# Attention backward on one core: first loads split over two queues, the second head's projections moved forward, dwq and dx tiles reordered

## The chip, the cores and the metric

The kernel runs on one NeuronCore of a Trainium2 chip. A core has a matrix engine (TensorE, PE in the profile, with its weight loads as PEld), a vector engine (VectorE, DVE), an activation engine (ScalarE, ACT), GpSimd (POOL), and SyncE (SP), which here only issues DMAs. Each engine runs its own instructions in the order in which the program puts them and waits on semaphores for the others. Sixteen DMA engines move data between HBM and the on-chip memory; DMAs are issued from the queue of an engine. TensorE writes to PSUM, which here is a pool of eight banks; VectorE or ScalarE evict the banks.

The metric is the device time of one execution in microseconds (us), the median of several runs. Lower is better.

## The reference

Two independent attention layers A and B, each with x (8 batches x 96 tokens x 640), a key and a value cache (8 x 32 heads x 512 x 128), and weights wq (640 x 4096) and wo (4096 x 640). All tensors are bfloat16. What is computed is the output and the gradient of all ten inputs:

```python
q = (x @ wq).reshape(B, Sq, H, Dh).transpose(0, 2, 1, 3)
scores = jnp.einsum("bhqd,bhkd->bhqk", q, k_cache) * (Dh ** -0.5)
p = softmax(scores, axis=-1)
o = jnp.einsum("bhqk,bhkd->bhqd", p, v_cache)
y = o.transpose(0, 2, 1, 3).reshape(B, Sq, H * Dh) @ wo
# out = concat([y_A, y_B], axis=-1); vjp of out with grad_out gives dx, dk, dv, dwq, dwo of A and of B
```

## The kernel before, in words

**Blocks, heads, batches.** Layer A is block 0, layer B is block 1. In a block the kernel goes through 32 heads, in a head through 8 batches; a pair of head and batch is one step of the inner pipeline. All work is put into an emitter with a tick and a slot, sorted by both, and only then issued. Head `h` of a block starts at tick `c0t = tick0 + 8*h` (tick0 is 13 for A and 269 for B); the text calls `c0t + k` the tick at offset k of that head. A framework adds the semaphores and may move an instruction a little within what the data allow; SyncE's DMAs and GpSimd's work are pinned to the program's order, except the very first loads.

**The inner pipeline (one step per tick).** `c_ld` loads K and V of two batches; `c_xt` transposes them by DMA, or, for the first heads, `c_s1` transposes K on TensorE. `c_s2a`: scores `S_ps` on TensorE, their negated row maximum `negm` on VectorE. `c_s2b`: exponential `E_sb` on ScalarE with the row sums. `c_s3a`, `c_s3b`: reciprocal `rinv` on VectorE, `P_sb` on GpSimd. A tick later P is transposed (`x_ps<-ident,P_sb`), evicted by ScalarE (`PT_sb`), and `dV_ps` is made; then the head's output (`x_ps<-PT_sb,V_sb`), `dP_ps` and `dl_ps`, from which VectorE makes `dS_sb`; then the transposes of dS (`dst_ps`), evicted by VectorE (`dST_sb`), `dK_ps`, and `x_ps<-dST_sb,K_sb` for dQ. ScalarE evicts `dK_sb`, `dV_sb`, `PT_sb` and the head's O and dQ (`OD`). In the profile the start of `S_ps` marks a tick: there are 512 of them.

**Work by head, laid between the batches.** `pA`, `pA2` load wq (two heads at once) and wo. `pB` transposes wo and wq of the head on TensorE (`woT_ps`, `wqT_ps`; woT is evicted by ScalarE, wqT by VectorE). `pC(h, 0, si)` is the projection Q and `pC(h, 1, si)` the projection of the gradient (`dOT_h`), each in a piece of 512 and one of 256 tokens, five matmuls a piece (`q_ps`). `pD` transposes them by batch (`n_ps`, to `dOnat_h` and `Qnat_h`). `qA` transposes O and dQ back (`nat_ps`, to `Onat` on ScalarE, 768 columns, and `dQnat` on VectorE). `qB` makes dwo from Onat, in two pieces of six matmuls, one evicted by ScalarE, one by VectorE. `qD` makes dwq of a pair of heads: five units of 6 matmuls of 256 columns (`dwq_ps`), each evicted by VectorE into `dwq_sb`, which has one buffer, and stored by `qD_st` one tick after the last unit. `gU` adds up the output (`which` 0) and dx (`which` 1) over groups of five heads, in six token tiles t of a 512- and a 128-column piece; in B the last group has two heads, and its dx tiles are written to `gT` and stored one by one (tiles 0 and 2 go by ScalarE and GpSimd, the rest by VectorE).

**Where the five dwq units go** is planned: every piece of work by head adds its TensorE time, less 0.8 of its ScalarE time, to its tick's planned load, and a pair `h` (odd) puts each unit at the least loaded offset of 18 to 29 from its head, at most two in one (lines 639 to 649). The last pair of a block has fixed offsets.

**The start** (block A, head 0). SyncE's queue issues x tiles 0 to 3 as one DMA, wo of head 0, wq of heads 0 and 1, K, x tiles 4 and 5, g in two DMAs, then V and K. TensorE runs 32 warm-up matmuls, transposes x tiles 0 to 3, wo and wq, projects Q, and so on; g's six transposes come after the first S.

Of the kernel before, what the change touches and what calls it, by code (L numbers as in the profile page):

```python
# [11 lines left out]
BF16 = mybir.dt.bfloat16  # L12
# [30 lines left out]
SL_HEAD = 90  # L43
# [3 lines left out]
OFF = dict(ldk=-5, ldv=-4, kt=-3, vt=0, s2=3, s3=3, s4=4, s5=5, s6=6, s7=7, s8=8)  # L47
HK = dict(pA=-10, pA2=-9, pB=-3, pC0=[-2, 0], pC1=[-1, 0], pD1=1, pD0=2, qA0=18, qA1=17, qA1e=21, qDw=(18, 29), qB=[19, 20], qD=[(18, 0, 2), (19, 2, 4), (21, 4, 5)])
# [8 lines left out]
def build_block(tc, em, tick0, blk, x, kc, vc, wq, wo, g_all, out_all, dx, dk, dv, dwq, dwo, ident, ones, pools, HG=6, first=True, groups=None):  # L57
    nc = tc.nc
    B, Sq, D = x.shape
    _, H, Sk, Dh = kc.shape  # L60
    assert Dh == 128 and Sk % 128 == 0 and D % 128 == 0
    T = B * Sq
    assert T % 128 == 0
    TT = T // 128
# [10 lines left out]
    NG = len(groups)  # L75
    GH0 = [sum(groups[:i]) for i in range(NG)]
    tsplits = []
    t0 = 0
# [17 lines left out]
    wq_v = wq.rearrange("(c p) n -> p c n", p=128)  # L96
    dwq_v = dwq.rearrange("(c p) n -> p c n", p=128)

    const, ps, kvp, wk, hd, hst, grp = (pools[k] for k in ("const", "ps", "kvp", "wk", "hd", "hst", "grp"))

    def bank(shape, dt, name):
        return ps.tile(shape, dt, name=name, tag="bank")

    S = {}
# [9 lines left out]
    def pinned(ins):  # L114
        return tc.keep_in_program_order(ins)
# [25 lines left out]
    def setup_nat(which_, t0, t1):  # L141
        def f():
            key = "x_nat" if which_ == 0 else "g_nat"
            src_flat = x_flat if which_ == 0 else g_flat
            if t0 == 0:
                S[key] = const.tile([128, TT, D], BF16, name=key, bufs=1)
            nc.sync.dma_start(S[key][:, t0:t1], src_flat.rearrange("(t p) d -> p t d", p=128)[:, t0:t1])
            if first and which_ == 0 and t0 == 0:
                pA2(0)()
                pA(0)()  # L150
        return f
# [6 lines left out]
    def evac(eng, dst, src, sc=None):  # L158
        if eng == "act":
            nc.scalar.activation(dst, src, ACT.Identity, scale=(1.0 if sc is None else sc))  # L160
        else:
            if sc is None:
                nc.vector.tensor_copy(dst, src)  # L163
            else:
                nc.vector.tensor_scalar(dst, src, float(sc), None, op0=ALU.mult)
# [21 lines left out]
    def pA(h):  # L187
        def f():
            start = first and h == 0
            if h % 2 == 0:  # L190
                wq_p = hd.tile([128, DC, 256], BF16, name="wq_p", bufs=2)
                with nc.allow_non_contiguous_dma(reason="wq slice of two heads"):
                    if start:
                        nc.sync.dma_start(wq_p[:], wq_v[:, :, h * 128:(h + 2) * 128])
                    else:
                        pinned(nc.sync.dma_start(wq_p[:], wq_v[:, :, h * 128:(h + 2) * 128]))
            else:
                wq_p = HS[(blk, h - 1)]["wq_p"]
            HS.setdefault((blk, h), {}).update(wq_p=wq_p, wq_h=wq_p[:, :, (h % 2) * 128:(h % 2 + 1) * 128])
        return f  # L200

    def pA2(h):
        def f():
            wo_h = hst.tile([128, D], BF16, name="wo_h", bufs=HG + 3)
            ld = nc.sync.dma_start(wo_h[:], wo[h * 128:(h + 1) * 128, :])
            if not (first and h == 0):
                pinned(ld)
            HS.setdefault((blk, h), {})["wo_h"] = wo_h
        return f

    def pB(h):
        def f():
            st = HS[(blk, h)]
            woT_ps = bank([128, DC * 128], BF16, "woT_ps")
            for c in range(DC):
                nc.tensor.transpose(woT_ps[:, c * 128:(c + 1) * 128], st["wo_h"][:, c * 128:(c + 1) * 128], ident[:])  # L216
            woT_h = hd.tile([128, DC * 128], BF16, name="woT_h", bufs=1)
            evac(EV["pB0"], woT_h[:], woT_ps[:])
            st["woT_h"] = woT_h
            wqT_ps = bank([128, DC * 128], BF16, "wqT_ps")  # L220
            for c in range(DC):
                nc.tensor.transpose(wqT_ps[:, c * 128:(c + 1) * 128], st["wq_h"][:, c, :], ident[:])  # L222
            wqT_h = hst.tile([128, D], BF16, name="wqT_h")
            evac(EV["pB1"], wqT_h[:], wqT_ps[:])
            st["wqT_h"] = wqT_h
            st["slot"] = (blk * H + h) % OD.shape[2]
            st["OT_h"] = OD[:, 0, st["slot"]]
            st["dQT_h"] = OD[:, 1, st["slot"]]
            st["QT_h"] = hd.tile([128, T], BF16, name="QT_h")
            st["dOT_h"] = hd.tile([128, T], BF16, name="dOT_h")  # L230
        return f

    def pC(h, which, si):
        def f():
            st = HS[(blk, h)]
            (t0, w) = tsplits[si]
            if which == 0:
                dst = st["QT_h"]
                lhs = lambda c: st["wq_h"][:, c, :]
                rhsT = S["xT"]  # L240
                sc = scale
            else:
                dst = st["dOT_h"]
                lhs = lambda c: st["woT_h"][:, c * 128:(c + 1) * 128]
                rhsT = S["gT"]
                sc = None
            q_ps = bank([128, w], F32, "q_ps")
            for c in range(DC):
                nc.tensor.matmul(q_ps[:], lhs(c), rhsT[:, c, t0:t0 + w], start=(c == 0), stop=(c == DC - 1))  # L249
            evac(EV["pC%d%d" % (which, si)], dst[:, t0:t0 + w], q_ps[:], sc)  # L250
        return f
# [249 lines left out]
    def qD_st(h):  # L501
        def f():
            with nc.allow_non_contiguous_dma(reason="dwq slice of two heads"):
                pinned(nc.sync.dma_start(dwq_v[:, :, (h - 1) * 128:(h + 1) * 128], HS[(blk, h)]["dwq_sb"][:]))
        return f
# [48 lines left out]
    def gU_st(which, t):  # L554
        def f():
            dst_flat = out_flat if which == 0 else dx_flat
            pinned(nc.sync.dma_start(dst_flat[t * 128:(t + 1) * 128, :], S.pop(("ob", which, t))))
        return f
# [7 lines left out]
    for g in range(NG):  # L566
        h0 = GH0[g]
        for hh in range(groups[g]):
            h = h0 + hh
            c0t = tick0 + h * B  # L570
            if not (first and h == 0):
                em.add(c0t + HK["pA"], SLOTS["LOAD"] + 1.7, pA(h))
                em.add(c0t + HK["pA2"], SLOTS["LOAD"] + 1.7, pA2(h))
            em.add(c0t + HK["pB"], SL_HEAD, pB(h), pe=558, act=713)
            fh = first and h == 0
            p0, p1, d1, d0, late = HK["pC0"], HK["pC1"], HK["pD1"], HK["pD0"], 0
            if fh:
                p0, p1, d1, d0, late = [-2, 3], [3, 3], 3, 3, 6.5
            elif h == 0:
                p0, p1, d1, d0, late = [-2, 2], [0, 3], 3, 4, 7  # L580
            for si in range(NTS):
                em.add(c0t + p0[min(si, 1)], SL_HEAD + (6.2 if fh and si == 1 else 0), pC(h, 0, si), pe=1090 if si == 0 else 546, act=522 if si == 0 else 420)
                em.add(c0t + p1[min(si, 1)], SL_HEAD + late, pC(h, 1, si), pe=1090 if si == 0 else 546, act=621 if si == 0 else 0)
            em.add(c0t + d1, SL_HEAD + (8 if late else 0), pD(h, 1), pe=446)
            em.add(c0t + d0, SL_HEAD + (9 if fh else 0), pD(h, 0), pe=446)
# [36 lines left out]
        cLg = tick0 + (h0 + groups[g] - 1) * B + B - 1  # L622
        gs0 = max(3, (GSPREAD0 * groups[g]) // HG)
        gs1 = max(3, (GSPREAD1 * groups[g]) // HG)
        if not first and g == NG - 2:
            gs0, gs1 = 9, 9
# [4 lines left out]
        for i, (which, t, gi) in enumerate(subs):  # L631
            if which == 0:
                tk = cLg + OFF["s5"] + 2 + (i * gs0) // n_out
            else:
                tk = cLg + OFF["s8"] + 2 + gs0 - 3 + ((i - n_out) * gs1) // n_out
            em.add(tk, SL_GRP, gU(g, which, t, gi), pe=groups[g] * gsplits[gi][1] / 2.4, act=440 if g == 0 else 0)
            if g == NG - 1 and gi == len(gsplits) - 1:
                em.add(tk + 1, SLOTS["LOAD"] + 1.6, gU_st(which, t))
    for h in range(1, H - 1, 2):
        c0t = tick0 + h * B  # L640
        ticks = []
        for _ in range(DC):
            k_ = min((k for k in range(HK["qDw"][0], HK["qDw"][1] + 1) if ticks.count(k) < 2), key=lambda k: em.load.get(c0t + k, 0.0))
            em.load[c0t + k_] = em.load.get(c0t + k_, 0.0) + 655
            ticks.append(k_)
        ticks.sort()
        for k_ in sorted(set(ticks)):
            em.add(c0t + k_, SL_HEAD + 2, qD(h, ticks.index(k_), ticks.index(k_) + ticks.count(k_)))
        em.add(c0t + ticks[-1] + 1, SLOTS["LOAD"] + 1.6, qD_st(h))
    pools["c_s45"] = c_s45  # L650
    pools["c_s8"] = c_s8
    return tick0 + H * B
# [121 lines left out]
```

## Time and profile before

| | |
|---|---|
| Time, median of 3 runs | 1628.04 us (1626.72 to 1629.08) |
| Profiled execution, its own time | 1626.66 us |
| Its span, first to last instruction | 1624.5 us |
| TensorE busy | 1611.3 us (99%) |
| ScalarE busy | 1392.7 us (86%) |
| VectorE busy | 1268.3 us (78%) |
| GpSimd busy | 528.6 us (33%) |
| Mean DMA rate | 280 GB/s |
| Granted TensorE clock | 1.000 |

How to read it: times in the profile count from the start of the span. A line of the timeline gives start, duration, engine, line of the kernel, operation, what it writes and reads, and in brackets how long the engine had been idle and what ended that. The lines of TensorE are pipelined, so that a row of it lasts longer than the distance to the next; the distance between starts is what it costs. SPq is SyncE's queue issuing a DMA. A list of waits gives the total, the count and the longest.

### The profile page before, as it was taken

The numbers are of one execution on the slowest core, as the hardware profiler recorded it, in microseconds if no ns is written. First come the engines' busy times: TensorE is split into PE (matmuls) and PEld (weight loads), VectorE is DVE, ScalarE is ACT, GpSimd is POOL, SyncE is SP. The second block draws the span as 40 slices with busy tenths as digits, with TensorE's granted clock in tenths as the row PEclk, the third lists the DMA queues.
The fourth block names the chain that finished last, engine by engine and source line by source line (L and its number), as shares of the span: only waits on it lengthen the run. The fifth ranks groups of instructions, "written<-read, shape, count | busy, mean of one in ns | idle before, by whom it ended". The sixth has DMA issues, their size and how long they took to land.

```text
span 1624.5 us, 55213 instructions
## 1 busy us (share of the span) xinstructions
PE 1611.3 (99%) x21048; PEld 1284.3 (79%) x21048; DVE 1268.3 (78%) x2904; ACT 1392.7 (86%) x3521; POOL 528.6 (33%) x1034
## 2 busy tenths in 40 slices
PE   8999999999999999999999999999999999999999
PEld 7887787787788787877878877877877877877876
DVE  6886687778788788788888767778878878777886
ACT  7999898798898797988869988978978977987985
POOL 2333333233333233333323323323333333332332
PEclk9999999999999999999999999999999999999999
DMA  9999999999999999999999999999999999999994
GB/s 270 285 285 286 271 288 294 280 275 287 287 288 290 269 284 281 268 283 295 299 286 287 290 290 283 296 293 271 274 290 274 288 286 271 283 285 281 288 275 146
DMA packets 875626, 454.96 MB, mean 280 GB/s; under 512 B 548192, under 2 KB 875360, under 8 KB 875360
## 3 DMA queue, kind: packets, MB, share of 16 engines
q1 hardware_dynamic: 875360, 451.43, 113.3%
q8 instruction: 165, 2.70, 0.7%
q14 instruction: 101, 0.83, 0.1%
HBM read 161.09 MB, written 159.12 MB: 197 GB/s over the span
## 4 chain that ended last, share of the span: by engine, by line
PE 94%; DVE 2%; ACT 1%; DMA 1%; issue 1%; SPq 0%; POOL 0%; DVEq 0%; ACTq 0%; POOLq 0%
PE q_ps L249 13%; PE o_ps L520 12%; PE dK_ps L438 7%; PE dV_ps L395 7%; PE dP_ps L423 7%; PE S_ps L304 7%; PE dwo_ps L475 6%; PE dwq_ps L496 6%; PE dst_ps L352 5%; PE x_ps L371 5%; PE x_ps L365 5%; PE x_ps L346 5%; PE n_ps L264 3%; PE nat_ps L461 3%; PE woT_ps L216 1%; PE wqT_ps L222 1%
## 5 line engine op out<-in xcount | busy, mean ns | idle before, releaser
L335 POOL TENSOR_SCALAR P_sb<-E_sb,rinv 96x512 bf16<-96x512 bf16 x512 | 354.3, 692 | 1069.2 <-DVE rinv L326 1033.7
L316 ACT ACTIVATE E_sb<-S_ps,negm 96x512 bf16<-96x512 f32 x512 | 356.5, 696 | 113.2 <-DVE negm L306 107.7
L427 DVE SCALAR_TENSOR_TENSOR dS_sb<-dP_ps,dl_ps,P_sb 96x512 bf16<-96x512 f32 x512 | 382.8, 748 | 42.1 <-PE dl_ps L425 35.5
L441 ACT ACTIVATE dK_sb<-dK_ps 128x512 bf16<-128x512 f32 x512 | 307.5, 601 | 87.0 <-PE dK_ps L438 85.9
L306 DVE TENSOR_REDUCE negm<-S_ps 96x1 f32<-96x512 f32 x512 | 347.6, 679 | 37.8 <-PE S_ps L304 36.8
L398 ACT ACTIVATE dV_sb<-dV_ps 128x512 bf16<-128x512 f32 x512 | 316.3, 618 | 0.0
L384 ACT ACTIVATE PT_sb<-x_ps 128x384 bf16<-128x384 bf16 x512 | 258.2, 504 | 0.0
L520 PEld LDWEIGHTS <-OD 128*128 128x128 bf16 x1536 | 135.2, 98 | 102.6 <-issue 2.0
L395 PE MATMUL dV_ps<-dOnat_h,P_sb 96*128 96x128 bf16 x2048 | 197.9, 219 | 0.4 <-DVE dOnat_h L163 0.4
L438 PE MATMUL dK_ps<-Qnat_h,dS_sb 96*128 96x128 bf16 x2048 | 197.8, 219 | 0.0
L423 PE MATMUL dP_ps<-VT,dOT_h 128*96 128x512 bf16 x512 | 195.3, 381 | 0.3
L326 DVE RECIPROCAL rinv<-rowsum 96x1 f32<-96x1 f32 x512 | 80.3, 157 | 145.1 <-ACT E_sb L316 141.8
L354 DVE COPY dST_sb<-dst_ps 128x384 bf16<-128x384 bf16 x512 | 177.7, 347 | 16.9 <-PE dst_ps L352 16.9
L413 POOL TENSOR_TENSOR prod<-OD,dOT_h 128x96 bf16<-128x96 bf16 x512 | 186.6, 365 | 8.5 <-ACT OD L381 7.9
L304 PE MATMUL S_ps<-KT,QT_h 128*96 128x512 bf16 x488 | 184.6, 378 | 0.4
L381 ACT ACTIVATE OD<-x_ps 128x192 bf16<-128x192 f32 (+1 forms) x515 | 173.4, 337 | 4.6 <-PE x_ps L346 3.7
L352 PE MATMUL dst_ps<-ident,dS_sb 96*128 96x96 bf16 x2048 | 172.2, 206 | 0.5 <-ACT PT_sb L384 0.3
L371 PE MATMUL x_ps<-ident,P_sb 96*128 96x96 bf16 x2048 | 171.7, 205 | 0.9 <-POOL P_sb L335 0.8
L365 PE MATMUL x_ps<-PT_sb,V_sb 128*128 128x96 bf16 x2048 | 172.1, 206 | 0.3 <-ACT PT_sb L384 0.2
L346 PE MATMUL x_ps<-dST_sb,K_sb 128*128 128x96 bf16 x2048 | 170.7, 206 | 0.0
L346 PEld LDWEIGHTS <-K_sb 128*128 128x128 bf16 x2048 | 135.2, 98 | 38.1
L496 PE MATMUL dwq_ps<-dQnat,x_nat 128*128 128x256 bf16 x960 | 142.0, 272 | 0.0
(76 smaller groups left out, 3060.0 us busy)
## 6 DMA issues: line engine op xcount, KB each, us to landing
out_dram<-dV_sb SPq DMA_DIRECT2D x256, 256.0 KB, 3.6
out_dram<-dK_sb SPq DMA_DIRECT2D x256, 256.0 KB, 3.5
K_sb<-in_A_k_cache_dram SPq DMA_DIRECT2D x128, 256.0 KB, 4.1
V_sb<-in_A_v_cache_dram SPq DMA_DIRECT2D x128, 256.0 KB, 4.0
K_sb<-in_B_k_cache_dram SPq DMA_DIRECT2D x128, 256.0 KB, 4.0
V_sb<-in_B_v_cache_dram SPq DMA_DIRECT2D x128, 256.0 KB, 3.9
out_dram<-dwo_sb SPq DMA_DIRECT2D x64, 160.0 KB, 3.2
out_dram<-dwq_sb SPq DMA_DIRECT2D x32, 320.0 KB, 4.3
```

The source lines that it names most:

```text
L304: nc.tensor.matmul(S_ps[:], hs["QT_h"][:, tok], st["KT"], start=True, stop=True)
L306: nc.vector.tensor_reduce(negm[:], S_ps[:], axis=AX.X, op=ALU.max, negate=True)
L316: nc.scalar.activation(E_sb[:], st["S_ps"][:], ACT.Exp, bias=st["negm"][:], scale=1.0, accum_out=rowsum[:])
L335: pinned(nc.gpsimd.tensor_scalar(P_sb[:], st["E_sb"][:], st["rinv"][:], 0.0, op0=ALU.mult, op1=ALU.add))
L346: nc.tensor.matmul(dQT_ps, st["K_sb"][:, c, :], st["dST_sb"][:, c * Sq:(c + 1) * Sq], start=(c == 0), stop=(c == KC - 1))
L395: nc.tensor.matmul(dV_ps[:, c * 128:(c + 1) * 128], P_sb[:, c * 128:(c + 1) * 128], hs["dOnat_h"][:, b * 128:(b + 1) * 128], start=True, s ...
L398: nc.scalar.activation(SB[(blk, h, b // 2, "v")][:, b % 2], dV_ps[:], ACT.Identity, scale=1.0)
L423: nc.tensor.matmul(dP_ps[:], hs["dOT_h"][:, tok], st["VT"], start=True, stop=True)
L427: nc.vector.scalar_tensor_tensor(dS_sb[:], dP_ps[:], dl_ps[:, 0:1], st["P_sb"][:], op0=ALU.subtract, op1=ALU.mult)
L438: nc.tensor.matmul(dK_ps[:, c * 128:(c + 1) * 128], dS_sb[:, c * 128:(c + 1) * 128], hs["Qnat_h"][:, b * 128:(b + 1) * 128], start=True, s ...
L441: nc.scalar.activation(SB[(blk, h, b // 2, "k")][:, b % 2], dK_ps[:], ACT.Identity, scale=1.0)
L520: nc.tensor.matmul(o_ps[:], src[:, t * 128:(t + 1) * 128], rhs, start=(hh == 0), stop=(hh == groups[g] - 1))
```

## The change

Four edits, all of order:

- x tiles 0 to 3 are loaded by one DMA each; wo of head 0 and wq of heads 0 and 1 are issued from ScalarE's queue, where they stand ahead of its table load.
- Head 1 of block A: its first Q piece is put before g's transposes, its transposes of wo and wq, its other Q piece and the projections of the gradient each some ticks earlier. `QT_h` and `dOT_h` are now allocated where they are first written.
- In the last group of block B, dx tiles 2 to 4 come in one tick and tile 5 in the next; in the issued order dx tiles 0 to 4 stand ahead of the last dwq, and tile 5 behind it. Before, tiles 0 to 3 stood ahead.
- The planner's lowest offset for dwq is no longer always 18: it is at least six ticks behind the tick that stores the pair before.

What the last edit does to the planned offsets of the five units, for all pairs that differ:

| Pairs (block: h) | before | after |
|---|---|---|
| A: 3, 13; B: 3, 13, 23 | 18 19 21 21 27 | 20 21 21 24 27 |
| A: 7, 17, 25; B: 7, 17, 27 | 18 21 25 26 29 | 21 25 26 27 29 |
| A: 9, 19; B: 9, 19 | 19 21 22 25 28 | 21 22 25 25 28 |
| A: 11, 21; B: 11, 21 | 18 21 25 26 29 | 19 21 25 26 29 |
| B: 29 | 19 22 22 25 25 | 22 22 25 25 26 |

Offset 18 of pair h is offset 2 of head h+2. On ScalarE and GpSimd the order of instructions is otherwise unchanged after head 1; on SyncE two dwq stores change places with a neighbour.

```diff
@@ setup_nat
-            nc.sync.dma_start(S[key][:, t0:t1], src_flat.rearrange("(t p) d -> p t d", p=128)[:, t0:t1])
+            src = src_flat.rearrange("(t p) d -> p t d", p=128)
+            if first and which_ == 0 and t0 == 0:
+                for t in range(t0, t1):
+                    nc.sync.dma_start(S[key][:, t], src[:, t])
+            else:
+                nc.sync.dma_start(S[key][:, t0:t1], src[:, t0:t1])
@@ pA
-                        nc.sync.dma_start(wq_p[:], wq_v[:, :, h * 128:(h + 2) * 128])
+                        nc.scalar.dma_start(wq_p[:], wq_v[:, :, h * 128:(h + 2) * 128])
@@ pA2
-            ld = nc.sync.dma_start(wo_h[:], wo[h * 128:(h + 1) * 128, :])
-            if not (first and h == 0):
-                pinned(ld)
+            if first and h == 0:
+                nc.scalar.dma_start(wo_h[:], wo[h * 128:(h + 1) * 128, :])
+            else:
+                pinned(nc.sync.dma_start(wo_h[:], wo[h * 128:(h + 1) * 128, :]))
@@ build_block, heads
-            em.add(c0t + HK["pB"], SL_HEAD, pB(h), pe=558, act=713)
             fh = first and h == 0
+            f2 = first and h == 1
+            em.add(c0t + (-5 if f2 else HK["pB"]), SL_HEAD + (9.5 if f2 else 0), pB(h), pe=558, act=713)
...
+            elif f2:
+                p0, p1 = [-5, -4], [-3, 0]
...
-                em.add(c0t + p0[min(si, 1)], SL_HEAD + (6.2 if fh and si == 1 else 0), pC(h, 0, si), pe=1090 if si == 0 else 546, act=522 if si == 0 else 420)
+                em.add(c0t + p0[min(si, 1)], SL_HEAD + (6.2 if fh and si == 1 else (5.5 if f2 and si == 0 else 0)), pC(h, 0, si), pe=1090 if si == 0 else 546, act=522 if si == 0 else 420)
@@ build_block, groups
                 tk = cLg + OFF["s8"] + 2 + gs0 - 3 + ((i - n_out) * gs1) // n_out
+                if not first and g == NG - 1:
+                    tk = cLg + OFF["s8"] + 2 + gs0 - 3 + (2 if t == TT - 1 else (1 if t > 1 else 0))
@@ build_block, dwq
+    lo_ = HK["qDw"][0]
     for h in range(1, H - 1, 2):
...
-            k_ = min((k for k in range(HK["qDw"][0], HK["qDw"][1] + 1) if ticks.count(k) < 2), key=lambda k: em.load.get(c0t + k, 0.0))
+            k_ = min((k for k in range(lo_, HK["qDw"][1] + 1) if ticks.count(k) < 2), key=lambda k: em.load.get(c0t + k, 0.0))
...
         em.add(c0t + ticks[-1] + 1, SLOTS["LOAD"] + 1.6, qD_st(h))
+        lo_ = max(HK["qDw"][0], ticks[-1] + 1 - 2 * B + 6)
```

More of the change, by code (lines that the diff above doesn't have):

```diff
@@ L228, in f @@
             st["dQT_h"] = OD[:, 1, st["slot"]]
-            st["QT_h"] = hd.tile([128, T], BF16, name="QT_h")
-            st["dOT_h"] = hd.tile([128, T], BF16, name="dOT_h")
         return f
@@ L236, in f @@
             (t0, w) = tsplits[si]
+            key = "QT_h" if which == 0 else "dOT_h"
+            if key not in st:
+                st[key] = hd.tile([128, T], BF16, name=key)
             if which == 0:
```

## The prediction

> **What bounds the kernel now.** First the head of the page, then its chain: TensorE holds 94% of it, at the full granted clock. ScalarE is next at 86%.
>
> ```profile
> span 1624.5 us, 55213 instructions
> PE 1611.3 (99%) x21048; PEld 1284.3 (79%) x21048; DVE 1268.3 (78%) x2904; ACT 1392.7 (86%) x3521; POOL 528.6 (33%) x1034
> PE 94%; DVE 2%; ACT 1%; DMA 1%; issue 1%; SPq 0%; POOL 0%; DVEq 0%; ACTq 0%; POOLq 0%
> ```
>
> The change adds and removes no arithmetic. Its time can come only from places where TensorE waits, so I looked for these: in the windows by stage (core 0: us, PE, PEld, DVE, ACT, POOL busy, clock, DMA), in the waits, and in the timeline.
>
> ```profile
> 0.00:5.00 5.00, 3.42 (x32) 3.25 (x32) 0.22 (x2) 1.28 (x1) 0.70 (x6) 1.00 0.54 169
> 5.00:10.00 5.00, 4.44 (x54) 3.31 (x54) 2.82 (x6) 3.10 (x5) 0.00 (x0) 1.00 1.07 371
> 15.00:20.00 5.00, 3.97 (x57) 3.18 (x55) 3.68 (x8) 2.99 (x9) 0.69 (x1) 1.00 0.93 251
> 20.00:25.00 5.00, 4.14 (x49) 2.90 (x48) 3.64 (x11) 4.41 (x13) 2.05 (x5) 1.00 1.17 331
> 35.00:40.00 5.00, 4.35 (x58) 3.11 (x57) 4.52 (x13) 4.31 (x13) 1.86 (x4) 1.00 0.95 247
> ```
>
> Some 5 us of TensorE are idle in the first 40. The DMA engines are full from 5 us on; ScalarE is near 90% from 20 us on. The timeline names two of the waits, one on data, one on GpSimd:
>
> ```profile
> 10.13 1.85 PE L137 MATMUL tp_ps<-ident,g_nat 128*128 128x128 bf16 x30 [0.53 <-DMA g_nat<-in_grad_out_dram]
> 21.21 0.34 PE L371 MATMUL x_ps<-ident,P_sb 96*128 96x96 bf16 x4 [0.81 <-POOL P_sb L335]
> ```
>
> After that there is one long wait in 1560 us (SyncE, VectorE, TensorE):
>
> ```profile
> 921.43 0.43 SPq L504 DMA_DIRECT2D out_dram<-dwq_sb  x1
> 925.50 0.42 DVE L165 TENSOR_SCALAR dwq_sb<-dwq_ps 128x256 bf16<-128x256 f32 x1 [2.15 <-DMA out_dram<-dwq_sb]
> 925.98 0.97 PE L475 MATMUL dwo_ps<-g_nat,Onat 128*128 128x320 bf16 x6 [1.78 <-DVE dwq_sb L165]
> ```
>
> `dwq_sb` has one buffer. The store of a pair leaves at 921.43 and lands 4.0 us later; the next pair's first eviction stands in VectorE's order until then, and TensorE stops behind it.
>
> The end, in order: last dwq (30 matmuls), dx tiles 4 and 5, their adds on VectorE.
>
> ```profile
> 1616.13 3.44 PE L496 MATMUL dwq_ps<-dQnat,x_nat 128*128 128x256 bf16 x30
> 1619.40 1.25 PE L520 MATMUL o_ps<-wqT_h,OD 128*128 128x512 bf16 x8
> 1620.03 1.68 DVE L526 SCALAR_TENSOR_TENSOR gT<-o_ps,dx_acc 128x512 bf16<-128x512 f32 x4 [2.82 <-PE o_ps L520]
> ```
>
> **The change, part by part.** Successive starts give the pace: a 512-column matmul 0.216 us, a 256-column one 0.109, a 128-column transpose 0.056. On ScalarE E, its accumulator read, dK, OD, PT and dV take 0.59+0.09+0.48+0.21+0.37+0.47 = 2.2 us a tick. The sum is made against the profiled execution, 1626.66 us (span 1624.5 and 2.16 around it), 1.38 below the median of 1628.04.
>
> *Start.* x's first four tiles land together at 5.08 (issue 0.74, 4.3 to landing). Split, tile 0 can be transposed when the warm-up ends at 4.51, and the last tile is what counts. SyncE issues three more DMAs of about 0.45 each, but loses wo and wq (0.49, 0.43), so K, x's rest and g leave one issue, about 0.45, later; their landing is set by bytes, which are the same, as the engines are full (371 GB/s). ScalarE gets two issues, about 0.9 us, ahead of its table load (1.28); its first eviction starts at 5.62 and covers both. The first projection then starts at about 6.75 instead of 7.01. Little of that survives: x's second transfer lands at 8.22 and g's at 10.08 whatever goes before.
>
> Head 1's first Q piece, 5 x 0.216 = 1.08 us, now fits from 9.3 to 10.4, half of it in the 0.53 wait for g; g's transposes start at 10.4 instead of 10.13. ScalarE does E of batch 0 at 10.16 instead of 11.22, then head 1's Q, then gT from 11.35 (before: 10.62). The first product of gT starts at about 12.65 (12.63): level, with 1.08 us done ahead. Then woT, wqT and the second Q piece (0.55+0.55) go between batches 1 and 2. There VectorE's new order puts batch 1's reciprocal behind batch 2's row maximum: 19.1 instead of 17.14. GpSimd makes P at 19.3 to 20.0, and TensorE, which used P at 18.27, waits till 20.05, about 1.4 us. This new wait takes the place of those at 16.68 (0.42), 17.67 (0.61) and 21.21 (0.81). S of batch 4 comes at about 22.75 instead of 22.07, 0.68 late, with 1.08+1.08+0.55 = 2.71 us done ahead. The next two ticks lack that work and run at ScalarE's 2.2 us; S of batch 6 comes at about 27.2 (28.13) with equal work left. **-0.8 us.** Ends: -2.0 (2.71-0.68, if ScalarE kept up) and +0.3 (x's last tile late).
>
> [...] No row of before has a second queue.
>
> *Spread of dwq.* The new lower bound keeps a pair's first dwq six ticks behind the tick that stores the pair before. The wait at 925.98 goes: the pair's first unit moves from tick +18 to +20, about 4 us on, and the store has landed. **-1.8**; ends -1.9 and 0, if it reappears elsewhere.
>
> But 20 pairs change, and in 15 places a unit of 6 matmuls (0.655 us) leaves one kind of tick, offset 2 of an odd head, which also evicts the 768-column Onat on ScalarE. Offset 2 of head 2 has the same other work and no unit, so before shows what such a tick does; head 9 is one of the 15. S_ps starts, three ticks each, other TensorE work equal:
>
> ```profile
> 51.92 0.38 PE L304 MATMUL S_ps<-KT_pe,QT_h 128*96 128x512 bf16 x1
> 59.36 0.38 PE L304 MATMUL S_ps<-KT,QT_h 128*96 128x512 bf16 x1
> ```
> ```profile
> 219.72 0.38 PE L304 MATMUL S_ps<-KT,QT_h 128*96 128x512 bf16 x1
> 227.38 0.38 PE L304 MATMUL S_ps<-KT,QT_h 128*96 128x512 bf16 x1
> 224.23 0.68 ACT L316 ACTIVATE E_sb<-S_ps,negm 96x512 bf16<-96x512 f32 x1 [0.21 <-DVE negm L306]
> ```
>
> Head 2 needs 7.44 us; head 9 needs 7.66, 7.01 without its unit. So the light tick costs 0.43. The ledger at head 9 agrees. Without the unit S comes 0.5 earlier, but ScalarE's Onat holds it till 223.9: E starts there instead of 224.23. Reciprocal and dS queue behind E on VectorE, and TensorE's dst transposes wait 0.23 in the next tick, 0.15 in the one after, less the 0.05 of slack they had: 0.33. Of the 15, six are like that (heads 9, 19, 27 of block A; 9, 19, 29 of B): 6 x 0.33 = 2.0. Five have a unit two ticks on, which hides the second wait: 5 x 0.2 = 1.0. Four get the unit back in the very next tick: 0. **+3.0**; ends 0 (ScalarE's 0.2 idle covers it) and 15 x 0.43 = 6.4. The ticks that receive a unit have waits near 0.01 and gain nothing. Later `dwq_sb` stores and evictions follow their units.
>
> *End.* Tile 4 (2 x 0.216 + 2 x 0.056 = 0.54) goes ahead of dwq; its adds run at 17.2 to 18.1, in VectorE's 2.82 idle. dwq ends 0.54 later; its store leaves at 20.55 instead of 20.01 and lands, at the 2.4 of this store in before, at 22.95. Tile 5's adds start at 20.57 and end at 21.46 instead of 21.71. **-0.25**; ends -0.5 and +1.3 (dwq's store taking its mid-kernel median of 4.3). SyncE's four earlier dx stores end at 19.27, so tile 4's is out of the way.
>
> Sum: -0.8 - 1.8 + 3.0 - 0.25 = +0.15, or 1626.8 for such an execution, 1628.2 as a median.
>
> **The rivals.** *Light ticks cost next to nothing and the start keeps more.* For: ScalarE had 0.21 idle before that E, and the start's 2.0 is only lost if ScalarE lags. Against: head 2. Light ticks 0.6, start -2.0: -2.0-1.8+0.6-0.25 = -3.45, 1624.6, faster.
>
> *Light ticks cost what head 2 shows, everywhere.* Place: TensorE's dst and P transposes at the 15. 15 x 0.43 = 6.4 against 2.85 gained: +3.6, 1631.6, slower. It decides from 0.41 per tick on. Against: nine of the 15 get work back at once.
>
> *The change does not remove the stall:* SyncE issued that store some 12 us behind the pair's last eviction (908.76), so its lag, not the tick, may decide. Another pair waits: +1.95, 1630.0, no change that can be told.
>
> **How the numbers follow.** A measurement of this kernel tells about 0.2%, 3.3 us. Forecast 0.57 (own range 1626 to 1630.5); first rival 0.24; second 0.12; third 0.07. Faster 0.24, same 0.64, slower 0.12. The range 1624.0 to 1631.4 reaches to both outer rivals.
>
> **What would show it.** In the changed profile: no wait of dwo_ps on dwq_sb; S of batch 4 near 22.8 and of batch 6 near 27; a wait on P_sb near 20; in head 9 TensorE waits of 0.2 and 0.15 before dst_ps; tile 5's adds ending 0.25 nearer to dwq's start. I am wrong if the light ticks show no new waits, or if dwq's store lands last.

## The result, and the profile after

The changed kernel takes 1630.74 us (median of 20 executions, 1627.56 to 1635.1), the kernel before beside it 1627.55 (20, 1625.65 to 1631.99). The ratio is 1.002, 95% interval 1.0011 to 1.0029: a little slower, right at what a measurement of this kernel can tell. The forecast was 1628.2, in a range of 1624.0 to 1631.4: the median lies inside the range, but outside the forecast case's own 1626 to 1630.5.

The profiled execution of after is its fastest, 1627.56 us with a span of 1625.8. That is 0.9 above before's profiled execution (span 1.2 longer), while the medians are 3.2 apart. So there are two questions: where the 1.2 us of the profile come from, and what the other executions have besides.

Of the page of after, its head and its chain (TensorE 82% instead of 94%, since the chain now leads through ScalarE in places; 166 of 21048 matmul records are missing from this trace, so its busy sum over the span says nothing against before's):

```profile
span 1625.8 us, 55084 instructions
PE 1604.1 (99%) x20882; PEld 1284.3 (79%) x21048; DVE 1272.1 (78%) x2900; ACT 1389.9 (85%) x3521; POOL 526.7 (32%) x1034
PE 82%; ACT 9%; issue 3%; DVE 3%; DMA 2%; POOL 0%; SPq 0%; ACTq 0%; DVEq 0%; POOLq 0%
```

The windows of after at the stretches shown of before (us, PE, PEld, DVE, ACT, POOL busy, clock, DMA share, GB/s):

```profile
0.00:5.00 5.00, 3.91 (x37) 3.92 (x38) 0.22 (x2) 1.28 (x1) 0.70 (x6) 1.00 0.62 184
5.00:10.00 5.00, 4.59 (x51) 3.27 (x51) 2.28 (x5) 3.27 (x5) 0.00 (x0) 1.00 1.05 365
15.00:20.00 5.00, 3.91 (x54) 3.14 (x53) 3.86 (x9) 2.81 (x8) 0.00 (x0) 1.00 0.98 278
20.00:25.00 5.00, 3.78 (x46) 2.76 (x48) 2.97 (x8) 4.11 (x11) 2.73 (x5) 1.00 1.11 301
35.00:40.00 5.00, 4.42 (x66) 3.39 (x64) 4.52 (x12) 4.10 (x12) 1.18 (x3) 1.00 0.87 218
```

TensorE starts sooner (3.91 instead of 3.42 us busy in the first 5) but loses it again from 15 to 25 us (7.69 instead of 8.11 busy). The timeline of TensorE in after shows how:

```profile
6.08 0.89 PE L137 MATMUL tp_ps<-ident,x_nat 128*128 128x128 bf16 x10 [0.33 <-DMA x_nat<-in_A_x_dram]
7.55 1.25 PE L256 MATMUL q_ps<-xT,wq_p 128*128 128x512 bf16 x4
11.06 1.84 PE L137 MATMUL tp_ps<-ident,g_nat 128*128 128x128 bf16 x30
18.72 0.42 PE L311 MATMUL S_ps<-KT_pe,QT_h 128*96 128x512 bf16 x1 [0.48 <-DVE KT_pe L300]
20.77 0.34 PE L378 MATMUL x_ps<-ident,P_sb 96*128 96x96 bf16 x4 [1.24 <-POOL P_sb L342]
23.51 0.40 PE L311 MATMUL S_ps<-KT_pe,QT_h 128*96 128x512 bf16 x1
24.52 0.34 PE L359 MATMUL dst_ps<-ident,dS_sb 96*128 96x96 bf16 x4 [0.40 <-DVE dS_sb L434]
```

The first projection starts at 7.55, not at 6.75: x's last tile is late. It lands at 6.46, behind wq (5.83); before's single DMA landed all four at 5.09. g's transposes no longer wait for g, and start at 11.06 (before 10.13). The wait for P of batch 1 is there, as worked out. S of batch 12, where the two kernels do the same again, starts at 44.04 instead of 43.37.

At the store of `dwq_sb`, the timeline of after:

```profile
921.44 0.42 SPq L511 DMA_DIRECT2D out_dram<-dwq_sb  x1
926.05 0.84 PE L482 MATMUL dwo_ps<-g_nat,Onat 128*128 128x320 bf16 x5
930.46 0.41 DVE L170 TENSOR_SCALAR dwq_sb<-dwq_ps 128x256 bf16<-128x256 f32 x1
```

The store leaves at the same time, but the next eviction into `dwq_sb` now comes at 930.46 and waits for nothing. In head 9, one of the light ticks, ScalarE in after:

```profile
224.37 0.82 ACT L165 ACTIVATE Onat<-nat_ps 128x768 bf16<-128x768 bf16 x1
225.06 0.71 ACT L323 ACTIVATE E_sb<-S_ps,negm 96x512 bf16<-96x512 f32 x1
```

E follows Onat with no idle time (0.21 in before): ScalarE now bounds this tick. And the end of after:

```profile
1615.12 3.07 PE L527 MATMUL o_ps<-wqT_h,OD 128*128 128x512 bf16 x20
1618.03 3.44 PE L503 MATMUL dwq_ps<-dQnat,x_nat 128*128 128x256 bf16 x30
1621.30 0.71 PE L527 MATMUL o_ps<-wqT_h,OD 128*128 128x512 bf16 x3
1621.94 0.89 DVE L533 SCALAR_TENSOR_TENSOR gT<-o_ps,dx_acc 128x512 bf16<-128x512 f32 x2 [2.56 <-PE dwq_ps L503]
```

Only tile 5 is left behind dwq. From the starts of S_ps in both traces (after less before, at the same tick) the profile's 1.23 us are: start +0.67; light ticks without the pair at the store +2.25 (a unit that moves behind the last S counted back); that pair (its light tick and the store wait together) -1.41; end -0.13; and -0.15 of small differences elsewhere.

### The profile page after: what moved, and what is told of

Same layout as the page of the kernel before. It is cut to its first block, busy times and chain, and to the rows that moved or that the text cites. A ratio compares the mean times of both kernels' runs of the same rounds, so it can differ in the third digit from the quotient of the medians.

```text
span 1625.8 us, 55084 instructions
## 1 busy us (share of the span) xinstructions
PE 1604.1 (99%) x20882; PEld 1284.3 (79%) x21048; DVE 1272.1 (78%) x2900; ACT 1389.9 (85%) x3521; POOL 526.7 (32%) x1034
## 4 chain that ended last, share of the span: by engine, by line
PE 82%; ACT 9%; issue 3%; DVE 3%; DMA 2%; POOL 0%; SPq 0%; ACTq 0%; DVEq 0%; POOLq 0%
PE o_ps L527 12%; PE q_ps L256 10%; PE dwq_ps L503 6%; PE dwo_ps L482 6%; PE S_ps L311 6%; PE dK_ps L445 6%; PE dV_ps L402 6%; PE dP_ps L430 6%; PE dst_ps L359 4%; PE x_ps L378 4%; PE x_ps L372 4%; PE x_ps L353 4%; ACT E_sb L323 3%; PE n_ps L271 3%; PE nat_ps L468 2%
```

## The experiments

The kernel before ran beside each, and its median there is the one given. One number recurs: the *lag*, the time from the end of the second `dK_sb` eviction of two batches to the issue of their store on SyncE, worked out from the timelines. It grows in the second block from 4.5 us at 820 us to between 13 and 17 at 920 us, in every trace. A lag alone makes no wait: in before it is 14.4 at 255 us too, and TensorE waits for nothing there. `KT` is K transposed by DMA; a wait for it is called a KT wait.

### One part of the change at a time

**First part alone** (x in four DMAs; wo and wq of head 0 from ScalarE's queue):

```diff
-                        nc.sync.dma_start(wq_p[:], ...)
+                        nc.scalar.dma_start(wq_p[:], ...)
-            ld = nc.sync.dma_start(wo_h[:], ...)
+            if first and h == 0:
+                nc.scalar.dma_start(wo_h[:], ...)
...
```

> The kernel before with only the first part: x's first four tiles in four transfers, wo and wq of head 0 on ScalarE's queue. Theory (the two queues share the DMA engines, so x's last tile lands behind wq): first projection at about 7.55 us instead of 7.01, g's transposes no earlier than 10.6, S of batch 6 about 28.6 instead of 28.13, time +0.5 us. Rival (my forecast): first projection at 6.75, g's transposes at 10.1, time 0 to -0.3 us. On the medians: after stood 3.2 us above before there, but only 1.2 us in the profiled span, and 10 of its 20 executions showed a granted clock of 0.998 or 0.999; if these dips come with this part, its executions show them and those of before beside it do not.

Measured: 1626.22 against 1628.12, ratio 0.9994 (0.9985 to 1.0003). Its timeline:

```profile
7.67 1.25 PE L255 MATMUL q_ps<-xT,wq_p 128*128 128x512 bf16 x4
10.10 1.11 PE L137 MATMUL tp_ps<-ident,g_nat 128*128 128x128 bf16 x17
```

The first projection is late, as the theory had it, but g's transposes are not: in before TensorE stands 0.53 us for g, here the lateness takes up that wait, and S of batch 12 starts at 43.31 (43.37). The part by itself costs nothing that the times can tell. What it does to the first projection has to be read over all traces. In the four with the split, x's last tile lands at 6.46 to 6.72 us instead of 4.99 to 5.14, and the first projection follows 1.1 later, at 7.55 to 7.81. In the ten with x in one DMA it comes at 6.92 to 7.64 (median 7.05), and there it goes by TensorE's pace: its successive transposes are 0.107 us apart up to a moment between 3.83 and 6.43 us, and 0.056 from then on. Where that moment lies at 5.03 or before (five traces) the projection comes by 7.01; where it lies at 6.20 and 6.43, at 7.47 and 7.64. So the split makes the projection late by about 0.5, and in some executions the late change of pace does the same without it.

**Second part alone** (head 1's transposes and projections between the first batches):

```diff
+            f2 = first and h == 1
+            em.add(c0t + (-5 if f2 else HK["pB"]), SL_HEAD + (9.5 if f2 else 0), pB(h), pe=558, act=713)
...
+            elif f2:
+                p0, p1 = [-5, -4], [-3, 0]
...
```

> The kernel before with only the second part: head 1's transposed weights and projections between the first batches. Theory A (the parts add up: after lost 0.67 us up to batch 12, 0.54 of it in the first projection, so this part loses the rest): S of batch 6 at about 28.25 instead of 28.13, time +0.1 us. Theory B (my forecast's working for this part, which uses the 0.53 us wait for g that is there again when x lands early): S of batch 6 at about 27.2 to 27.6, time -0.5 to -0.9 us. Both expect a wait of TensorE for P of batch 1 of 1.2 to 1.4 us near 20 us, in place of 0.81 at 21.21.

Measured: 1628.62 against 1628.12, ratio 1.0006 (0.9998 to 1.0015). S of batch 6 starts at 28.44, S of batch 12 at 43.97 (+0.60): theory A's figures, but not for its reason, as the first projection came at 7.47 in this execution with x in one DMA (one of the two with the late change of pace). 0.46 of the 0.60 is that lateness. In before it is swallowed by the wait for g (the first part's run shows that); here head 1's Q piece stands in that place, nothing is left to swallow it, and it runs through to the end. Without it the part would stand at +0.14, which is an estimate, and still not at theory B's -0.5 to -0.9. The wait for P was 1.24, as both theories had it.

**Third part alone** (the lower bound on dwq's offsets):

```diff
+    lo_ = HK["qDw"][0]
-            k_ = min((k for k in range(HK["qDw"][0], HK["qDw"][1] + 1) ...
+            k_ = min((k for k in range(lo_, HK["qDw"][1] + 1) ...
+        lo_ = max(HK["qDw"][0], ticks[-1] + 1 - 2 * B + 6)
```

> The kernel before with only the third part: the lower bound on a pair's first dwq tick. Theory: the wait on the store of dwq_sb at 925.98 us is gone (-1.8 us), and the 15 ticks that lose a unit cost 2.8 us, 0.4 where the unit comes two ticks later, 0.18 where it comes further on, 0 where it comes in the next tick: together +1.0 us. Rival: the light ticks' loss was due to the other parts, which shift what ScalarE and GpSimd do: -1.8 us. If the clock dips of the executions of after come from this part, its executions show 0.998 or 0.999 more often than those of before beside it.

Measured: 1630.32 against 1628.12, ratio 1.0017 (1.0008 to 1.0026): this part carries the loss. The profiled execution has the light ticks as in after, no store wait, and another wait in its place. TensorE's waits from 900 to 945 us, and two windows:

```profile
PE S_ps L304 <- DMA KT<-K_sb: 3.7, 2, 3.3
```
```profile
928.00:932.00 4.00, 1.09 (x9) 0.59 (x7) 1.32 (x3) 1.70 (x6) 1.02 (x2) 1.00 1.25 164
932.00:936.00 4.00, 3.60 (x31) 3.02 (x32) 1.54 (x4) 1.52 (x4) 0.67 (x1) 0.57 1.15 295
```

SyncE's lag is 16.9 us at 918 to 923 (after: 13.0 to 13.7; why the two differ is not shown). The transpose of K is issued at 926.00 and lands 6.4 us later; TensorE stands for 3.3 us and then gets a clock of 0.5 for 3.4 us, which costs 1.7 more (an estimate from these two numbers). Neither of the two theories of this run had that.

**Fourth part alone** (five of six dx tiles ahead of the last dwq):

```diff
+                if not first and g == NG - 1:
+                    tk = cLg + OFF["s8"] + 2 + gs0 - 3 + (2 if t == TT - 1 else (1 if t > 1 else 0))
```

> The kernel before with only the fourth part: five of six dx tiles ahead of the last dwq. Theory: the last instruction ends 0.13 to 0.25 us earlier against the start of the last dwq's neighbours, as VectorE ends tile 5's adds earlier; time -0.1 to -0.3 us. Rival: the last dwq's store, which now leaves 0.54 us later, lands last: 0 to +1.3 us.

Measured: 1627.87 against 1628.12, ratio 1.0001 (0.9992 to 1.0009). In the trace the difference to before shrinks from 2.57 at the last batches (0.75 from a store wait near 122 us, 2.0 from waits on K's transpose and on the store at 909 to 929, which this part doesn't touch) to 2.37 at the end: -0.20. Too little for the times to show.

Two of these theories asked whether a part brings the low mean clocks seen in after. None does by itself: they lie below 1.000 in 3 of 11 executions of the first part, 6 of the second (one at 0.998), 4 of the third and 3 of the fourth, and in 16 of 33 of before beside them.

### The change again, and without its third part

> The changed kernel once more, for a second profiled execution. In the first one SyncE stood 13.7 us behind at 923 us (from the end of a pair's last dK eviction to the issue of its store) and TensorE had no wait there. With the third part alone SyncE stood 16.9 us behind and TensorE waited 3.7 us for KT, and the granted clock was then 0.5 for 3.4 us. Theory (SyncE's lag decides, and differs from execution to execution): median 1630 to 1631.5, and in this profile either a lag near 14 us, no KT wait and 1627.5 to 1628.5 us, or a lag of 16 us or more with a KT wait of 2 to 4 us and 1631 to 1635 us. Rival (the first profile is typical and its 1.2 us over before is the whole difference): no KT wait again, median at most 1.5 us above before beside it.

Measured: 1629.96 against 1627.69, ratio 1.0016 (1.0007 to 1.0026); the profiled execution 1629.78. Lag 13.6 to 14.2 near 920 us and no KT wait, as in the first one, and the light ticks cost the same. But S of batch 12 comes at 45.72, 2.35 later than in before. Two windows of it:

```profile
18.20:21.60 3.40, 1.68 (x20) 1.18 (x20) 1.73 (x6) 2.44 (x8) 1.25 (x2) 1.00 1.19 329
21.60:25.00 3.40, 3.40 (x22) 2.25 (x21) 1.18 (x3) 2.45 (x7) 0.89 (x3) 0.51 1.10 307
```

Up to 21.4 us it runs like the first execution, the 1.24 us wait on P included; then TensorE gets half the clock for 3.4 us. The theory's median (1630 to 1631.5) is missed by 0.04 only, but it has the place wrong, as it asked for a lag and a wait at 920: of the 1.95 us of span over the first profile, 1.68 are there at batch 12, behind the new wait on P and the half clock that follows it. The rival had the missing KT wait right and the median too low: 2.3 above before, where it allowed 1.5 (the interval, 1.1 to 4.2, does not exclude that).

The change without its third part (`lo_` back to the fixed 18):

> The changed kernel without its third part: the lower bound on dwq's ticks is taken out, the other three parts stay. Theory (the third part carries the loss): the wait of dwo_ps for the store of dwq_sb near 926 us is back, 1.8 to 2.8 us, the light ticks are gone, and the time is that of before within 0.8 us (+0.6 from the start as in the changed kernel, -0.1 from the end). Rival (the start part carries part of it, or the parts do not add up): 1.5 to 2.5 us above before.

Measured: 1626.54 against 1627.69, ratio 0.9996 (0.9987 to 1.0004). The store wait is back, 1.1 us in this execution (1.8 to 2.8 expected); S of batch 12 is 0.95 late, and the span ends where before's does. As the theory had it: without the third part nothing is left that the times can show.

### Is it SyncE, the transfers, or the wait itself?

**Third part, with the stores of dwo on GpSimd's queue** (besides the third part's own edit):

```diff
-            pinned(nc.sync.dma_start(dwo[h * 128:(h + 1) * 128, :], ...))
+            pinned(nc.gpsimd.dma_start(dwo[h * 128:(h + 1) * 128, :], ...))
```

> The kernel before with the third part, and the stores of dwo issued by GpSimd instead of SyncE: 64 issues of about 0.5 us fewer on SyncE. Theory (SyncE's issue is the bound near 925 us): SyncE's lag there falls from 16.9 to 13 us or less, the KT wait and the half clock behind it do not come, and the time is 1 to 3 us below the 1630.3 of the third part alone: what is left above before is the light ticks' 2.8 less the store wait's 1.8 to 2.8. Rival A (the DMA engines' bytes are the bound, and who issues does not matter): lag and KT wait as before, time as the third part alone. Rival B (GpSimd is held by its issue, so that P comes late): TensorE waits for P_sb at the dwo ticks, time 2 to 10 us longer.

Measured: 1630.31 against 1627.69, ratio 1.0018 (1.001 to 1.0027), as the third part alone. Lag 15.7 to 16.0, KT wait 2.0, then half the clock for 3.4 us: rival A. GpSimd's issues show no harm on P: TensorE waits for it 0.8 us in the whole span, as in before.

**Before's order of dwq, with the stores of dwo and dwq on GpSimd's queue** (the same edit in `qB_st` and in `qD_st`):

> The kernel before with its own order of dwq, and the stores of dwo and dwq issued by GpSimd instead of SyncE. Theory (the wait near 926 us is SyncE's lag and nothing else): the store of the pair leaves within 1 us of its last eviction at 909, has landed by 914, TensorE does not wait, and no light tick is made: time 1.8 to 2.8 us below before, and less spread since no half-clock stretch follows. Rival A: the lag grows at another place and KT is waited for instead, time as before within 1 us. Rival B: GpSimd's issue holds P back, time 2 to 10 us longer.

Measured: 1628.91 against 1627.69, ratio 1.0009 (1.0000 to 1.0017). GpSimd's timeline and TensorE's waits from 900 to 945 us:

```profile
909.11 0.91 POOL L504 DMA_DIRECT2D out_dram<-dwq_sb  x1 [0.48 <-DVE dwq_sb L165]
```
```profile
PE S_ps L304 <- DMA KT<-K_sb: 2.0, 2, 1.5
```

The store that TensorE waited for in before leaves at 909.11 and lands 4.6 us later, 12 us before it is needed, and no light tick was made. Still TensorE waits 2.0 us there, now for K's transpose; SyncE's lag is 15.2. S_ps starts 0.36 earlier than in before ahead of this place and 0.29 later behind it, so the stretch lost 0.65 where 1.8 should have been gained: rival A. (The span is 2.4 us longer, though the last matmul starts only 0.21 later: with the last dwq store on its queue GpSimd's final drain lasts until 1626.15, 2.1 us longer than that store takes to land. Without these 2.2 us at the end, which is an estimate, the median would lie about 1 us below before, not the 1.8 to 2.8 of the theory.)

**The later dwq at one pair only**, the one with the wait:

```diff
-            k_ = min((k for k in range(HK["qDw"][0], ...
+            k_ = min((k for k in range(20 if not first and h == 3 else HK["qDw"][0], ...
```

> The kernel before with the later dwq at one pair only, the pair of heads 2 and 3 of the second block (first unit at tick +20 instead of +18), where before waits for the store near 926 us. Theory A (my forecast's -1.8): the store wait goes, one light tick costs 0.4, and the time is 1.4 to 2.4 us below before. Theory B (from the runs so far: the transfers are 15 to 17 us behind there, and what does not wait for the store waits for KT, as with the third part alone and with the stores on GpSimd): a KT wait of 1 to 3.5 us takes its place, time within 0.8 us of before.

Measured: 1630.01 against 1627.37, ratio 1.001 (1.0002 to 1.0019). Of its 12 executions five lie at 1626.6 to 1629.1 with a mean clock of 1.000, and seven at 1629.9 to 1631.6 with 0.999 or 0.998. The profiled one is of the lower group (1626.75), with this wait of TensorE near 929 us:

```profile
PE S_ps L304 <- DMA KT<-K_sb: 0.9, 1, 0.9
```

Of the forecast's -1.8 little is left: with the pair's light tick and this wait the stretch gains 0.43 (S_ps starts +0.64 against before ahead of it, +0.21 behind it). That is an execution without half clock. Theory B has the wait nearly right (0.9 for 1 to 3.5 us) and its time too low: by the interval the kernel is 0.3 to 3.1 us slower than before.

**Fewer bytes:** five stores of dwo left out.

```diff
+            if first or h > 4:
-            pinned(nc.sync.dma_start(dwo[h * 128:(h + 1) * 128, :], ...))
+                pinned(nc.sync.dma_start(dwo[h * 128:(h + 1) * 128, :], ...))
```

> The kernel before, which leaves out the stores of dwo of heads 0 to 4 of the second block (five transfers of 160 KB between 815 and 925 us; these rows of the output are not written). Theory (the DMA engines' backlog is the bound there; at about 290 GB/s these 0.8 MB are 2.8 us of it): the lag of SyncE's dK stores at 917 to 923 us falls from 15.7 to about 13, the store wait near 926 us falls to 0 and no KT wait comes: 1.5 to 2.8 us below before. Rival (a lag of SyncE's issue alone, as the stores moved to GpSimd were meant to relieve): five issues of 0.5 us, the lag falls by the same 2.5 us and the time too. What tells them apart is the run with dwo's and dwq's stores on GpSimd, where the issues left SyncE, the bytes stayed, and the lag stayed at 15.2.

Measured: 1626.66 against 1627.37, ratio 0.9997 (0.9988 to 1.0005). Lag 15.0 at 921 us instead of 15.7, and TensorE's wait there:

```profile
PE dwo_ps L475 <- DVE dwq_sb L165: 1.3, 1, 1.3
```

The direction is right, 0.5 us off the wait, but not the size. The test is weaker than its text says: in before only three of these five stores are issued ahead of 925 us (at 870, 896 and 918), the others at 944 and 968. Neither the bytes nor the issues of three stores, taken away alone, clear the backlog.

**K's transposes of four batches on TensorE**, two DMA transposes fewer:

```diff
-        return h == 0 or (first and h == 1)
+        return h == 0 or (first and h == 1) or (not first and h == 2 and b >= 4)
```

> The kernel before with the transposes of K of the last four batches of head 2 of the second block made by TensorE instead of two DMA transposes (four times 0.22 us on TensorE, four copies on VectorE). Theory: the lag at 917 to 923 us falls from 15.7 to 13 or less, the wait near 926 us goes without a KT wait behind it: -1.8 to -2.8 and no half-clock stretch, +0.9 for TensorE's transposes: 1 to 2 us below before. Rival: VectorE's copies (0.5 us each) and the single KT_pe buffer make TensorE wait in these four ticks, 0.5 us each: within 1 us of before.

Measured: 1626.10 against 1627.37, ratio 0.999 (0.9982 to 0.9999), and all 11 executions between 1625.07 and 1626.34. The lag falls at once (3.1 instead of 6.4 at 856 us) and is 14.3 instead of 15.7 at 922, not 13 or less. The four ticks cost 0.83 together, and the wait shrinks from 1.8 to

```profile
PE dwo_ps L475 <- DVE dwq_sb L165: 0.7, 1, 0.7
```

None of the 11 executions has a mean clock below 1.000 (9 of the 29 of before beside them have). This version is 0.1% faster than before, with an interval that just excludes 1. The size on the median, 1.3 us, is the theory's, but not by its sum: the wait went down by 1.1 and not by 1.8 to 2.8, and the profiled span is only 0.4 shorter than before's. Against the 20 executions of before at a mean clock of 1.000 (median 1626.92) the gain is 0.8; the rest goes with the executions at a low clock, which this version does not have.

**The third part on top of that:**

> The third part together with K's transposes of four batches on TensorE. Without the third part that kernel ran at 1626.1 us, all executions within 1.3 us, with 0.7 us of the store wait left. Theory (the third part costs its light ticks, 2.8 us, and the waits for KT come on top where the transfers are late): the store wait is gone and no KT wait longer than 0.5 us comes, no half-clock stretch, the light ticks cost 2.8 us as before: 1626.1 - 0.7 + 2.8 = 1628.2 us, close together. Rival A (the light ticks' price is part of the late transfers and goes with them): 1625.4 to 1626.1 us. Rival B (the relief is too small once TensorE does not wait at 926 us): KT waits and half clock in half of the executions, median 1630 us.

Measured: 1627.99 against 1627.62, ratio 1.0003 (0.9994 to 1.0012), 11 executions between 1627.71 and 1628.64, none with a mean clock below 1.000. TensorE's waits from 900 to 945 us:

```profile
PE S_ps L304 <- ACT E_sb L316: 0.2, 1, 0.2
```

Neither the store nor KT is waited for, and the kernel is 1.9 us slower than the one without the third part. With the 0.7 us of store wait that it saves, the light ticks' bare price is 2.6 (2.3 if each of the two kernels is set against before beside it, 3.0 from the spans of the two profiles). The theory's 1628.2 is met; rivals A and B fall.

## Why the prediction was right or wrong, step by step

**Start, forecast -0.8, measured +0.67 in the first profile and +2.35 in the second: this is the step that failed.** S of batch 6 was put at 27.2 and came at 28.52 (27.2 for 28.13 would have been -0.93; the sum has -0.8). Of the 1.32, 0.76 is there at S of batch 4 (23.51 for 22.75). It begins with the first projection, put at 6.75 ("the last tile is what counts") and seen at 7.55, because that tile landed 1.4 us later than before's four. Splitting x over four DMAs did not help with wo and wq on another queue: wq landed ahead of the last tile (5.83 and 6.46), and from 5 to 10 us the two queues of after moved 365 GB/s where the one of before moved 371. The 480 KB of wo and wq are 1.3 us at 371 GB/s, an estimate; in the traces with the split the tile landed at 6.46 to 6.72, 1.4 to 1.6 later than before's 5.09, and the projection came at 7.55 to 7.81. But "little of that survives" was wrong the other way: lateness is swallowed only while g is waited for, and the second part fills that wait. The four traces with the second part agree on this: S of batch 12 is late by what the first projection is late and 0.13 to 0.15 more (0.1 in the second profile, once the half clock's 1.7 is taken off), so that the second part itself gains nothing. The other 0.56 of the 1.32 is the pace of the next two ticks, put at ScalarE's 2.2 us a tick and seen at 2.5 (23.51 to 28.52): ScalarE had idle time there (0.28 at 25.13), and the chain over VectorE's dS was late (0.40 at 24.52, 0.30 at 26.83). Another 0.28 is lost behind batch 6, where equal work was expected to take equal time. The wait on P, put at "about 1.4 us" near 20, was 1.24 at 20.77: the mechanism was right. The half clock that came behind this wait in the second profile, and not in the first, was not in the sum; it added 1.7.

**Light ticks, forecast +3.0.** The total was near: 2.25 and 2.42 in the two profiles of after, where the forecast has 2.8 without the pair at the store, and 2.6 with it in the run made for it. That was luck in part, as the split was wrong. By kind, from the S_ps starts of five traces:

```
light tick                          forecast   measured
heads A 9, 19, 27; B 9, 19, 29        0.33      0.18 to 0.20 (A 27: 0.06 to 0.14; B 9 once 0.42)
heads A 5, 15; B 15, 25               0.2       0.34, 0.41, 0.25 to 0.30, 0.41
heads A 13, 23; B 13, 23              0        -0.04 to -0.01
```

In the first row the light tick and the one behind it lose 0.42 (0.25 and 0.17; the ledger had 0.38), but 0.24 comes back within the next ten ticks, which a ledger of two ticks did not follow. In the second, the pairs give up units in two ticks running (offsets 18 and 19, for 20 and 24), and I counted only the first; whatever its share, the unit at +20 does not hide the loss. The two errors partly cancel.

**Store wait, forecast -1.8.** Both profiles of after bear it out: the wait is gone, and nothing takes its place (-1.4 with the pair's own light tick). As a price of the change it was wrong. The third rival ("its lag, not the tick, may decide. Another pair waits", 0.07) was nearest: not another pair, but K's transpose waits, as four kernels without the store wait showed (3.7, 2.0, 2.0 and 0.9 us), and with half the clock behind it in two of the four. When the next transfer is late enough to be waited for is not settled: with the light ticks in place, the two profiles of after (lag 13.0 to 14.2) have no KT wait, and two others (lag 15.7 to 17.2) have one. What I read as the price of a buffer was the place where the backlog of transfers came out.

**End, forecast -0.25:** -0.13, -0.15 and -0.20 in the three profiles that tell, the right sign and size.

**The median.** The sum was made against one execution and carried over to the median with a constant. For an execution like before's profiled one the sum gave 1626.8; seen were 1627.56 and 1629.78. The 0.75 to the first is a miss of 1.47 at the start, less 0.24 in the other three terms, 0.15 elsewhere and 0.33 outside the span. The first profile is the fastest of 20, and the median lies 3.2 above it. Half-clock stretches are part of that: they are shown behind the wait on P (in after) and behind the KT wait (in the third part alone). One of 3.4 us costs 1.7 us (an estimate from half the clock), or 0.1% of the span, and of the 31 executions of after listed with their clock 5 have a mean of 0.998 and 11 of 0.999; of 112 of before, none has 0.998 and 42 have 0.999. The mean is a rough sign only, as half clock behind the last matmul counts too: the profiled execution with the third part and the stores of dwo on GpSimd's queue has 0.998 with one stretch and 1.96 us of that. Nor is it all: two of the executions above 1631 have 1.000, and at 1.000 the medians still lie 2.1 apart (1628.79 in 15 executions of after, 1626.72 in 70 of before). What those have besides the first profile's 1.2 us of span is not shown, as none but that one was profiled; KT waits, as in the third part alone, are a guess.

**The rivals.** The third's 1630.0 lies nearest to the median, and its mechanism is half of what was seen. The second (0.43 at each light tick, 1631.6) falls: no kind of light tick costs that much throughout. The first (light ticks 0.6, start -2.0) falls on both counts.

## What to carry to other kernels

A single long wait on one transfer was here, with SyncE's queue 13 to 17 us behind, where a backlog came out (1.8 us on the store in before, 0.9 to 3.7 us on KT in four kernels without that wait), and not a price that goes with the wait: before removing one, look how far behind the queue is, and what would be late next. Work that fills a wait also takes away the slack that absorbed late transfers ahead of it (S of batch 12 at 43.31 with the split of x alone, at 44.04 in after). And count all that a re-planned schedule takes from each tick, since a tick that loses TensorE work gains less than that work once another engine bounds it (here 0.41 of 0.655 us, and 0.24 with the tick behind it).

## What the runs showed of the hardware

*Half the clock after a short wait.* Every half-clock stretch between the first and the last matmul in these traces is 3.4 us long at 0.5 (the second profile of after has a clock of 0.51 from 21.60 to 25.00). One wait of 2.0 us had a stretch behind it (third part with the stores of dwo on GpSimd's queue), one of 2.6 us had none (first part alone). Two windows of 3.4 us, of the second part alone (first line, half clock from 927.8 on) and of the first part alone (second kernel, no half clock):

```profile
924.40:927.81 3.41, 1.37 (x26) 1.20 (x23) 1.00 (x3) 2.65 (x7) 0.00 (x0) 1.00 1.10 331
```
```profile
924.45:927.86 3.41, 1.37 (x11) 1.00 (x11) 1.44 (x5) 1.35 (x4) 0.99 (x2) 1.00 1.17 291
```

TensorE need not stand still all the while: in the 3.4 us ahead of the four stretches it was busy for 0.19 us (third part alone), 1.37 (second part alone), 1.41 (third part with the stores of dwo on GpSimd's queue) and 1.68 (second profile of after). As little work went without half clock, too: 1.37 us in the first part alone, above, and 1.68 in the first profile of after, from 18.20 to 21.60 as in the second, with a clock of 1.00 behind it. So a busy share of 0.4 to 0.5 went either way, and these busy times (their ends are modelled) do not make it sharper; what decides is not shown. A wait of 2 us thus cost 2 us or, with a stretch behind it, 3.7, which is an estimate from the 1.7 us that a stretch costs.

*The first microseconds.* The warm-up matmuls and the first transposes run at half the later pace (0.107 and 0.056 us) until a moment that differs by execution, 3.83 to 6.43 us from the start. The windows' clock column, which has 1.00 there, does not show it.

*A backlog that does not mind the queue.* Eight stores moved from SyncE to GpSimd took 4 us of issue off SyncE between 800 and 925 us and left its lag at 15.2 us (15.7). SyncE's other issues took longer instead: all of them together took 110.9 us in before and 109.9 without the eight. Two DMA transposes less took 1.4 off the lag, three stores of 160 KB left out 0.7. Whether the engines' bytes, the transposes' own rate or the issue is the last bound there is open.
